# Turning gated tiles by DMA in the spatial stage instead of on TensorE in the last stage

## The chip, the cores and the metric

The kernel runs on one core of a Trainium2 chip. The core has TensorE (PE in the profile; PEld is its weight load), VectorE (DVE), ScalarE (ACT), GpSimd (POOL) and SyncE (SP, which here only issues DMAs). ACT and POOL issue DMAs too. The metric is the device time of one execution in microseconds. Before the change it is 636.57 us, the median of 3 runs (636.25 to 636.86).

## The reference

All arithmetic is in float32; S = 2048 rows, D = 512, H = 32 heads of 16, Fh = 688. With xn the normalised rows of x, the result is x + A(xn) + B(xn):

```python
def _A_ref(x, wqkv, w_phi, wo):          # linear attention
    q, k, v = heads of x @ wqkv
    phi = lambda t: concat(softmax(t @ w_phi), softmax(-t @ w_phi))   # per head
    kv, z = sum_s phi(k) v, sum_s phi(k)
    o = phi(q) kv / (phi(q) z + 1e-6)
    return o @ wo

def _B_ref(x, w_in, w_sp, b_sp, w_out):  # gated MLP with spatial mixing
    z = gelu(x @ w_in)
    z1 = z[..., :Fh]
    z2 = layernorm(z[..., Fh:])
    g = w_sp @ z2 + b_sp[:, None]        # over the 2048 rows
    return (z1 * g) @ w_out
```

The change is in B, between the product z1 * g and its multiplication with w_out.

## The kernel before

**Tiles and precision.** Rows go in 16 tiles of 128. Nearly every float32 product is made of three matmuls: both operands are split into a rounded high part and a rest (`round_h` on ACT, `rest_l` on DVE), and `mm3` adds high x high, high x low and low x high in PSUM.

**Stages.** First the input projections, the attention features and sums, and z1 before its GELU, which is stored to DRAM (`z1_d`). Then z2 with GELU and norm, split into the right-hand operands B, which stay in SBUF. Then the *spatial stage*: g = w_sp @ z2, for 8 pairs of row tiles (i = 0 to 7), each with four blocks of the inner dimension (n = 4i to 4i + 3), by a seven-product scheme in place of eight. The products P1, P2, P6, P5, P7, P3, P4 run in this order in every block, six matmuls each, and accumulate over the four blocks in seven PSUM buffers. There are eight such buffers (`psg`, tag "g"), taken in turn, so the first product of the next pair has a free one and the second needs the one that P1 of this pair held.

**What feeds TensorE in that stage.** `load_a` (SP's queue, line 516) loads weights of a block three blocks ahead, `prep_a` makes its left-hand operands with ACT roundings and DVE sums and rests; two sets alternate.

**The gate of a pair.** When the pair's last block is issued, `drain` (line 704) reads the seven PSUM buffers into the tile `c`: one ACT copy first (line 709), seven DVE operations after it. `gate` (line 719) then takes the GELU of z1 in place on ACT (line 722), multiplies by `c` on DVE (724), and writes, for the 48 remainder columns that do not fill a tile of 128, a rounded part and a rest side by side (727 to 729). Two DMAs on POOL's queue store the pair to DRAM (`u_d`, line 731). `load_z1` (line 687, POOL's queue) fetches the z1 of the next pair. The tiles `z1`, `c` and `rh` come from the pool `gt` with one buffer per name, so a name's next tile waits for all readers of the last one. The gate of the last pair runs in the last stage, after the iteration `GATE_LAST = 8`, and its `c` comes from another pool.

**The last stage.** For each row tile: load the gated tile (SP, line 746), turn it in blocks of 128 columns on TensorE into PSUM (`gate_T`, lines 749 to 761: five blocks and the 96 remainder columns), split the result into high and rest, multiply by w_out (`project_u`, line 885), add the attention output times wo (`project_o`, line 898), add x, store. Two tiles make an iteration; the tiles of a following iteration are turned in the current one. DVE also finishes the attention features of later tiles here, and POOL's queue copies them (line 836).

**Order.** Within an engine, instructions stand in an order that a planner lays down when the program is built: it plays the program through with its own costs and starts what is ready, earlier program order first. `tc.issue_after(x)` keeps instructions behind x on the same engine. At run time every engine and every DMA queue takes its instructions strictly in that order.

Of the kernel before, what the change touches and what calls it, by code (L numbers as in the profile page):

```python
# [11 lines left out]
F32R = mybir.dt.float32r  # L12
AF = mybir.ActivationFunctionType
# [12 lines left out]
KF = FH // P  # L26
REM = FH - KF * P
# [10 lines left out]
def mixer(ctx: ExitStack, tc: tile.TileContext, x, x_t, wv, wqkT, phi_bd, wo, w_in, wst, b_r, w_out, out):  # L38
# [32 lines left out]
    u_d = dram.tile([NT, P, FH + REM], F32, name="u_d")  # L71
# [615 lines left out]
    def load_z1(i):  # L687
        t = gt.tile([P, 2, FH + REM], F32, tag="z1", name="z1t")
        for k in range(2):
            pool.dma_start(t[:, k, :FH], z1_d[2 * i + k])  # L690
        return t
# [27 lines left out]
    def gate(i, cb, z):  # L719
        cb, first, _ = cb  # L720
        with tc.issue_after(first):
            act.activation(z[:, :, :FH], z[:, :, :FH], AF.Gelu_apprx_tanh)
        zs = z[:, :, :FH].rearrange("p k (j f) -> p k j f", j=2)
        dve.tensor_tensor(zs, zs, cb.rearrange("p (k j) f -> p k j f", k=2), op=ALU.mult)
# [4 lines left out]
        dve.tensor_copy(z[:, :, rm], rh.bitcast(F32))  # L729
        for k in range(2):  # L730
            pool.dma_start(u_d[2 * i + k], z[:, k])  # L731
# [13 lines left out]
    def load_u(i, t):  # L745
        sp.dma_start(t.bitcast(F32), u_d[i])
        return t

    def gate_T(ps, tag, z, h, l, rt):
        pt = ps.tile([P, 4, P], F32, tag=tag, name="ptu")  # L750
        for c in range(4):
            pe.transpose(pt[:, c].bitcast(F32R), z[:, c * P:(c + 1) * P], ident_r)
        round_h(act, h[:, :4], pt)
        rest_l(l[:, :4], pt, h[:, :4])
        pt = ps.tile([P, 4, P], F32, tag=tag, name="ptu2")
        pe.transpose(pt[:, 0].bitcast(F32R), z[:, 4 * P:5 * P], ident_r)
        lasts[2] = pe.transpose(pt[:2 * REM, 1].bitcast(F32R), z[:, KF * P:KF * P + 2 * REM], ident_r).ins
        round_h(act, h[:, 4:], pt[:, :1])
        lasts[1] = rest_l(l[:, 4:], pt[:, :1], h[:, 4:])
        lasts[0] = act.activation(rt, pt[:2 * REM, 1], AF.Copy).ins  # L760
        return h, l, rt
# [4 lines left out]
    def first_gate(i):  # L766
        a, b = slot("u_uh", F32R), slot("ul_rt", F32R)
        u = load_u(i, a[:, :FH + REM])
        return gate_T(psg, "g", u, k_tiles(a[:, FH + REM:]), k_tiles(b[:, :KF * P]), b[:2 * REM, KF * P:(KF + 1) * P])

# [18 lines left out]
    for n in range(NC):  # L789
# [21 lines left out]
        if n == NC - 2:  # L811
            us = {1: load_u(1, slot("u1", F32R)[:, :FH + REM])}
# [12 lines left out]
    def fetch_u(i):  # L825
        return load_u(i, cw.tile([P, FH + REM], F32R, tag="u", bufs=4, name="u"))
# [11 lines left out]
    def gated(z, ps=None):  # L838
        return gate_T(*(ps or (pst, "tr")), z, wk.tile([P, KF, P], F32R, tag="uh", name="uh"),
                      wk.tile([P, KF, P], F32R, tag="ul", name="ul"), wk.tile([2 * REM, P], F32R, tag="rt", name="rt"))  # L840

    kvT = cw.tile([P, 2 * NG, QP], F32, name="kvT")
    with tc.issue_after(cb[1]), tc.issue_after(cb[2]):
        uT.append(gated(us.pop(1), (psg, "g")))
# [40 lines left out]
    def project_u(i, u):  # L885
# [5 lines left out]
        for ds, p in parts:  # L891
            for c in range(KF):
                mm3(p, (uh[:, c], ul[:, c]), tuple(w[:, ds] for w in wu[c]), c == 0, False)
            for w in wu[KF]:
                pe.matmul(p, rt, w[:, ds], start=False, stop=False)  # L895
# [12 lines left out]
    GATE_LAST = 8  # L908
# [24 lines left out]
    for i in range(0, NT, 2):  # L933
# [56 lines left out]
```

## Time and profile before

| | |
|---|---|
| Runs | 636.25 to 636.86 us, median 636.57 (3 runs) |
| Profiled execution | 636.23 us, span 634.5 us |
| Busy, whole span | PE 629.0, PEld 571.1, DVE 509.0, ACT 267.9, POOL 114.9 us |
| Granted TensorE clock | 1.00 |
| DMA | 103.95 MB, mean 164 GB/s |

A row of a timeline gives the start, the busy time, the engine, the source line, the operation, what it writes and reads, the number of instructions merged, and in brackets how long the engine had stood idle before and what ended that. Matmuls of one engine overlap in the records, since they are pipelined: their pace is read from the starts. Rows with a "q" behind the engine's name are issues of DMAs, and "us to landing" is from issue until the data are there. A source line can be a helper's: L45 is `round_h`, L49 is `rest_l`, L53 to L55 are the three matmuls of `mm3`.

### The profile page before, as it was taken

What the parts mean: (1) busy time and instruction counts of PE and PEld (TensorE: products, weight loads), DVE (VectorE), ACT (ScalarE), POOL (GpSimd) and SP (SyncE); (2) the same over time, 40 slices, a digit from 0 to 9 for tenths busy, and PEclk for the clock granted to TensorE, in tenths of its full rate; (3) what the DMA queues carried; (4) which work ended last, traced back from release to release, by engine and by line L of the source; (5) the groups of instructions that cost most, each with busy time, mean ns of one, the idle gap of its engine ahead of it and who ended that gap; (6) DMA issues with size and microseconds to landing.
All of it is one profiled execution on the core that took longest, in us unless ns stands there. A gap on an engine that the chain in (4) does not pass through costs nothing.

```text
span 634.5 us, 11639 instructions
## 1 busy us (share of the span) xinstructions
PE 629.0 (99%) x4471; PEld 571.1 (90%) x4471; DVE 509.0 (80%) x941; ACT 267.9 (42%) x447; POOL 114.9 (18%) x195
## 2 busy tenths in 40 slices
PE   9999999999999999999999999999999999999997
PEld 7888888888888999999999999999999888888886
DVE  5979989998888578889987869678695698989521
ACT  5623334332433437887453434434353423323330
POOL 4542231322101005441011010000100200101000
PEclk9999999999999999999999999999999999999999
DMA  9477676666544941002464352543548877775620
GB/s 334 150 170 163 181 186 142 190 154 151 178 136 112 298 153 67 2 1 68 145 191 131 121 180 71 174 132 119 184 143 275 267 267 283 243 263 219 205 67 35
DMA packets 41908, 103.95 MB, mean 164 GB/s; under 512 B 5404, under 2 KB 6940, under 8 KB 41852
## 3 DMA queue, kind: packets, MB, share of 16 engines
q1 hardware_dynamic: 28524, 58.37, 28.7%
q0 software_dynamic: 10736, 38.67, 21.3%
q10 hardware_dynamic: 2592, 6.16, 2.6%
q8 instruction: 35, 0.57, 0.4%
q14 instruction: 21, 0.17, 0.1%
HBM read 62.01 MB, written 26.50 MB: 139 GB/s over the span
## 4 chain that ended last, share of the span: by engine, by line
PE 96%; DVE 3%; issue 0%; ACT 0%
PE g L54 11%; PE g L55 11%; PE g L53 11%; PE proj L53 6%; PE zps L53 6%; PE proj L55 6%; PE proj L54 6%; PE zps L55 6%; PE zps L54 6%; PE pout L53 6%; PE pout L54 5%; PE pout L55 5%; PE ptq L863 1%; PE po L877 1%; PE kvps L319 1%; PE pout L895 1%
## 5 line engine op out<-in xcount | busy, mean ns | idle before, releaser
L54 PE MATMUL g<-B,A 128*128 128x344 f32 x448 | 143.3, 320 | 0.0
L53 PE MATMUL g<-B,A 128*128 128x344 f32 x448 | 143.2, 320 | 0.0
L55 PE MATMUL g<-B,A 128*128 128x344 f32 x448 | 143.0, 320 | 0.0
L54 PEld LDWEIGHTS g<-B,A 128*128 128x128 f32 x448 | 84.2, 188 | 0.0
L53 PEld LDWEIGHTS g<-B,A 128*128 128x128 f32 x448 | 84.2, 188 | 0.0
L55 PEld LDWEIGHTS g<-B,A 128*128 128x128 f32 x448 | 84.1, 188 | 0.0
L49 DVE TENSOR_TENSOR A<-S,A 128x512 fp32r<-128x512 f32 x64 | 43.8, 688 | 29.8 <-ACT A L45 29.0
L45 ACT ACTIVATE A<-S 128x512 fp32r<-128x512 f32 x64 | 40.2, 631 | 60.5 <-PE g L55 37.1
L113 ACT ACTIVATE e<-e,r_x 128x1024 f32<-128x1024 f32 x32 | 36.8, 1149 | 46.0 <-DVE e L112 44.1
L53 PE MATMUL proj<-wqk_h,xT 128*128 128x512 f32 x124 | 49.6, 400 | 0.0
L45 ACT ACTIVATE A<-wf 128x512 fp32r<-128x512 f32 x64 | 33.3, 520 | 37.3 <-PE g L55 32.9
L55 PE MATMUL proj<-wqk_h,xT 128*128 128x512 f32 x124 | 48.8, 394 | 0.0
L54 PE MATMUL proj<-wqk_l,xT 128*128 128x512 f32 x124 | 48.7, 393 | 0.0
L115 DVE TENSOR_REDUCE sm<-e 128x64 f32<-128x1024 f32 x32 | 38.6, 1212 | 9.7 <-ACT e L113 9.4
L53 PE MATMUL zps<-w_h,xT 128*128 128x344 f32 x128 | 41.8, 326 | 0.4 <-ACT z1f L143 0.3
L55 PE MATMUL zps<-w_h,xT 128*128 128x344 f32 x128 | 40.9, 319 | 0.0
L54 PE MATMUL zps<-w_l,xT 128*128 128x344 f32 x128 | 40.8, 319 | 0.0
L49 DVE TENSOR_TENSOR A<-wf,A 128x512 fp32r<-128x512 f32 x64 | 35.4, 553 | 2.9 <-ACT A L45 2.5
L731 POOL DMA_DIRECT2D u_d<-z1t x16 | 8.7, 547 | 133.7 <-DVE A L49 93.8
L53 PE MATMUL pout<-wu,uh 128*128 128x512 f32 (+1 forms) x80 | 31.6, 395 | 0.0
L143 ACT ACTIVATE z1f<-zps,r_x 128x344 f32<-128x344 f32 (+1 forms) x30 | 17.0, 566 | 33.8 <-PE zps L55 33.3
L54 PE MATMUL pout<-wu,uh 128*128 128x512 f32 (+1 forms) x80 | 30.4, 380 | 0.0
(203 smaller groups left out, 1485.1 us busy)
## 6 DMA issues: line engine op xcount, KB each, us to landing
wf<-in_wst SPq DMA_DIRECT2D x64, 256.0 KB, 3.4
e_d<-e POOLq DMA_DIRECT2D x16, 544.0 KB, 4.1
et<-e_d SPq DMA_DIRECT2D x16, 544.0 KB, 5.0
zacc<-e POOLq DMA_DIRECT2D x16, 512.0 KB, 4.9
er<-et POOLq DMA_DIRECT2D x12, 512.0 KB, 4.0
u_d<-z1t POOLq DMA_DIRECT2D x16, 368.0 KB, 4.4
u<-u_d SPq DMA_DIRECT2D x15, 368.0 KB, 3.0
z_d<-z1f ACTq DMA_DIRECT2D x16, 344.0 KB, 3.8
```

Of the source, the lines that this page charges most:

```text
L45: return act.activation(h, src, AF.Copy).ins
L49: return (eng or dve).tensor_tensor(l, src, h.bitcast(F32), op=ALU.subtract).ins
L53: pe.matmul(dst, ah, bh, start=start, stop=False)
L54: pe.matmul(dst, ah, bl, start=False, stop=False)
L55: return pe.matmul(dst, al, bh, start=False, stop=stop).ins
L113: softmax_pair.exp = act.activation(e, e, AF.Exp, scale=scale).ins
L115: dve.tensor_reduce(sm, heads(e), axis=AX.X, op=ALU.add)
L143: z1_raw.last = act.activation(z[:, k], p, AF.Copy, scale=r_x[:, s:s + 1]).ins
L319: ins = pe.matmul(kv_acc[k:k + QP, m // 4], vs[:, m * QP:(m + 1) * QP], e[:, m * HP:(m + 1) * HP], start=s == 0 and m < 4, stop=s == NT - ...
L731: pool.dma_start(u_d[2 * i + k], z[:, k])
L863: pe.transpose(pt[:, a, k].bitcast(F32R), src, ident_r)
L877: lasts[3] = pe.matmul(po[r][c * QP:(c + 1) * QP, j // NG], kvT[rows, j], fs[j // 2][rows, j % 2], start=True, stop=True).ins
```

## The change

The gated tile is turned before it is stored. A float32 value is taken as two 16-bit halves. In `gate`, two ACT copies separate the low and the high halves of both row tiles into two planes; the planes lie in the tile `c`, which has been read by then. For each of the two row tiles a transposing DMA on SP's queue (`dma_start_transpose`) turns the 12 blocks of 128 x 128 halves into a tile "T", a POOL copy interleaves the halves again into the z1 tile, and the store follows as before, on POOL's queue. The tile is padded with zeros from 736 to 768 columns (UP), by a POOL memset ahead of each z1 load. In the last stage a load brings the turned tile; `gate_T` with its six TensorE transposes per tile is replaced by `gate_parts`, which splits the loaded tile with one ACT rounding, one DVE rest and one ACT copy of the remainder. Two ordering hints change with it, and `GATE_LAST` goes from 8 to 6; there the planes of the last pair have a tile of their own.

```diff
+UP = (KF + 1) * P
...
-    u_d = dram.tile([NT, P, FH + REM], F32, name="u_d")
+    u_d = dram.tile([NT, P, UP], F32, name="u_d")
...
     def load_z1(i):
-        t = gt.tile([P, 2, FH + REM], F32, tag="z1", name="z1t")
+        t = gt.tile([P, 2, UP], F32, tag="z1", name="z1t")
+        pool.memset(t[:, :, FH + REM:], 0.0)
...
+    def halves(ap):
+        return ap.bitcast(U16).rearrange("p (n two) -> p two n", two=2)
+
-    def gate(i, cb, z):
+    def gate(i, cb, z, planes):
...
+        planes = planes.bitcast(U16).rearrange("p (k two n) -> p k two n", k=2, two=2)
         for k in range(2):
+            act.activation(planes[:, k], halves(z[:, k]), AF.Copy)
+        for k in range(2):
+            t = gt.tile([P, 2, KF + 1, P], U16, tag="T", name="uT")
+            sp.dma_start_transpose(t.rearrange("p two b t -> p (two b) t"), planes[:, k].rearrange("p two n -> p (two n)"))
+            pool.tensor_copy(halves(z[:, k]), t.rearrange("p two b t -> p two (b t)"))
             pool.dma_start(u_d[2 * i + k], z[:, k])
...
-    def gate_T(ps, tag, z, h, l, rt):
...
+    def gate_parts(u, h, l, rt):
+        full = slice(0, KF * P)
+        round_h(act, h, u[:, full])
+        lasts[1] = rest_l(l, u[:, full], h)
+        lasts[0] = act.activation(rt, u[:2 * REM, KF * P:], AF.Copy).ins
+        return k_tiles(h), k_tiles(l), rt
...
         if n % NQ == NQ - 1 and i < NP - 1:
-            gate(i, drain(i, g, gt.tile([P, 4, FC], F32, tag="c", name="c")), z)
+            c = gt.tile([P, 2 * UP], F32, tag="c", name="c")
+            gate(i, drain(i, g, c[:, :2 * FH].rearrange("p (a b) -> p a b", a=4)), z, c)
...
-    GATE_LAST = 8
+    GATE_LAST = 6
...
         if i + 3 < NT:
-            with tc.issue_after(lasts[3]):
-                nxt[i + 3] = gated(us.pop(i + 3))
+            nxt[i + 3] = gated(us.pop(i + 3))
...
-                gate(NP - 1, cb, z)
+                gate(NP - 1, cb, z, gt.tile([P, 2 * UP], F32, tag="pl", name="pl"))
```

More of the change, by code (lines that the diff above doesn't have):

```diff
@@ L745, in load_u @@
     def load_u(i, t):
-        sp.dma_start(t.bitcast(F32), u_d[i])
+        sp.dma_start(t, u_d[i])
         return t
-    def gate_T(ps, tag, z, h, l, rt):
[L750 to L761, printed above, removed]
+    def gate_parts(u, h, l, rt):
[4 more added lines that the diff above has]
+        return k_tiles(h), k_tiles(l), rt
     def k_tiles(ap):
```

21 lines of the change are left out of this document (11 added, 10 removed).

## The prediction

> **What bounds the kernel now.** I read the page first, then the busy time by stage, then TensorE in order of time around the operations that go, and last the three queues through which a gated tile passes. All durations are of the profiled execution: 636.23 us, of which 634.5 is its span; the median of the three runs, 636.57, lies 0.34 higher.
>
> ```profile
> span 634.5 us, 11639 instructions
> PE 629.0 (99%) x4471; PEld 571.1 (90%) x4471; DVE 509.0 (80%) x941; ACT 267.9 (42%) x447; POOL 114.9 (18%) x195
> PE 96%; DVE 3%; issue 0%; ACT 0%
> ...
> 381.50:408.00 26.50, 26.50 (x170) 26.50 (x169) 20.41 (x44) 10.88 (x19) 2.16 (x4) 1.00 0.43 135
> 568.00:585.00 17.00, 17.00 (x120) 13.79 (x119) 15.75 (x32) 6.36 (x13) 1.07 (x3) 1.00 0.62 228
> 585.00:602.00 17.00, 17.00 (x120) 13.76 (x119) 9.87 (x16) 5.12 (x12) 2.16 (x4) 1.00 0.66 228
> ```
>
> The last three rows are one pair of the spatial stage and two pairs of the last stage (busy us of PE, PEld, DVE, ACT, POOL, then granted clock, DMA share, GB/s). TensorE has no hole in either, at clock 1.00, and the chain of waits is 96% TensorE. So a matmul removed shortens the run by its slot, and anything that makes TensorE wait lengthens it in full. DVE in the last stage has 17.00 - 15.75 = 1.25 us a pair to spare, so a gain of more than that would be cut off there.
>
> **What is removed: 96 transposes, six for each of 16 tiles.** Matmuls overlap in the records, so I go by starts.
>
> ```profile
> 585.57 0.63 PE L895 MATMUL pout<-wu,rt 96*128 96x512 f32 x2
> 586.58 1.09 PE L877 MATMUL po<-f,kvT 64*32 64x256 f32 x32
> ...
> 590.96 0.40 PE L55 MATMUL pout<-wu,ul 128*128 128x512 f32 x1
> 591.19 0.63 PE L895 MATMUL pout<-wu,rt 96*128 96x512 f32 x2
> 591.65 0.46 PE L752 MATMUL ptu<-zb,u 128*128 128x128 f32 x4
> 591.95 0.25 PE L756 MATMUL ptu<-zb,u 128*128 128x128 f32 x1
> 592.03 0.23 PE L757 MATMUL ptu<-zb,u 128*96 128x128 f32 x1
> 592.10 0.47 PE L53 MATMUL pout<-woh,oT 128*128 128x512 f32 x1
> 592.41 0.39 PE L54 MATMUL pout<-wol,oT 128*128 128x512 f32 x1
> ...
> 619.47 0.63 PE L895 MATMUL pout<-wu,rt 96*128 96x512 f32 x2
> 620.03 1.09 PE L877 MATMUL po<-f,kvT 64*32 64x256 f32 x32
> ```
>
> A 512-column matmul takes a slot of 591.19 - 590.96 = 0.23 us. From the remainder pair at 591.19 to the second output matmul at 592.41 go 1.22 us; three slots alone are 0.69, so the six transposes cost 0.53, the slower first matmul behind them included. Where the attention products follow, 585.57 to 586.58 is 1.01; at 619.47, where nothing is left to turn, it is 0.56: 0.45. Half of the tiles are of each kind: 8 x 0.98 = **7.8 us saved**. That is 0.98 a pair, under DVE's 1.25, and ACT and DVE do one split in place of two, so I take it whole. The tiles now loaded are 768 columns wide instead of 736; those loads have a pair's time and cost nothing.
>
> **What is added, and where it lies.** In the spatial stage each pair gets two ACT copies into the planes, two transposing DMAs on SP's queue, two POOL copies back, and the stores wait for all that. None is on TensorE. But they form a ring: the z1 tile, the tile c (now also the planes) and the turned tile T exist once each, so the next pair's z1 load waits for this pair's stores, the second transpose waits for the first POOL copy, and the next drain's first write to c waits for the second transpose. What it runs through now:
>
> ```profile
> 382.26 0.46 ACT L709 ACTIVATE c<-g 128x344 f32<-128x344 f32 x1 [0.48 <-PE g L55]
> 390.05 1.58 DVE L724 TENSOR_TENSOR z1t<-z1t,c 128x1376 f32<-128x1376 f32 x1
> 394.92 0.20 DVE L729 COPY z1t<-rh 128x96 f32<-128x96 f32 x1
> 395.66 1.08 POOL L731 DMA_DIRECT2D u_d<-z1t  x2 [18.73 <-DVE A L49]
> 402.03 1.08 POOL L690 DMA_DIRECT2D z1t<-z_d  x2 [5.28 <-issue]
> 408.72 0.46 ACT L709 ACTIVATE c<-g 128x344 f32<-128x344 f32 x1 [0.48 <-PE g L55]
> ```
>
> ```profile
> 302.38 1.19 POOL L690 DMA_DIRECT2D z1t<-z_d  x2 [10.80 <-PE g L55]
> 303.04 0.44 ACT L709 ACTIVATE c<-g 128x344 f32<-128x344 f32 x1
> 308.01 1.36 ACT L722 ACTIVATE z1t<-z1t 128x1376 f32<-128x1376 f32 x1 [0.99 <-DMA z1t<-z_d]
> 314.18 1.58 DVE L724 TENSOR_TENSOR z1t<-z1t,c 128x1376 f32<-128x1376 f32 x1
> 317.65 0.20 DVE L729 COPY z1t<-rh 128x96 f32<-128x96 f32 x1
> ```
>
> The ring in terms, from the gate's multiply to the next: multiply to the last DVE copy's end 5.07 us (390.05 to 395.12), or 3.67 in the first pair (314.18 to 317.85), I take 4.4; to the first store's issue 0.54; stores to z1 load 6.37; load to GELU 5.63 (302.38 to 308.01, where GELU waited for the DMA); GELU 1.36. Sum 18.3 against a period of 408.72 - 382.26 = **26.46**: 8.2 us are free.
>
> Now the additions on this ring. ACT's first plane copy, 1536 columns: 1.36 x 1536/1376 = 1.5, plus 0.3 for half of a rounding ahead of it in ACT's order. Pad 0.1. One store issue less at the end, -0.5. Together 1.4. Then twice a transpose T and twice a POOL copy C, which the trace does not show:
>
> ```profile
> u<-u_d SPq DMA_DIRECT2D x15, 368.0 KB, 3.0
> raw<-nm_d POOLq DMA_DIRECT2D x11, 256.0 KB, 6.3
> ...
> L49 POOL TENSOR_TENSOR w_l<-wrow,w_h 128x688 fp32r<-128x688 f32 x4 | 6.7, 1677 | 4.0 <-ACT w_h L45 4.0
> L170 POOL MEMSET zacc<- 128x1024 f32 x1 | 0.9, 942 | 0.0
> L163 POOL TENSOR_SCALAR_AFFINE_SELECT mask<-mask 128x256 f32<-128x256 f32 x2 | 0.9, 449 | 0.1
> masks.py:199 POOL TENSOR_SCALAR_AFFINE_SELECT ident<-ident 128x128 f32<-128x128 f32 x1 | 0.3, 284 | 0.1
> ```
>
> T moves 384 KB. Not below 3.0, the plain load of 368 KB on the same queue; above, 6.3, the slowest group to land. I take 3.4, near the plain load, as queue and bytes are alike and two-byte pieces can only add. C is 1536 elements with one read and one write: at the memset's rate 1.4; at the two-input operation's 1536/688 x 1.68 = 3.7; by the two one-input rows 1.29 ns a column, 0.28 + 1408 x 0.00129 = 2.1, which I take as the nearest.
>
> The Trainium skill bears on T. "DMA: Bandwidth & Descriptors", section "Latency and other measured facts", gives 261 GB/s for transposing DMAs and section "Anatomy of one DMA" a fixed 2 us: an estimate of 3.5 for T, and by it the sum below would be 1.2 us higher. No trace here shows it.
>
> **The sum.** The ring becomes 18.3 + 1.4 + 2 x (3.4 + 2.1) = 30.7 us, 4.2 more than the period: the gate slips 4.2 us later with every pair. What does a late gate hold up? Not the stores' readers, they come much later, but c. With the multiply at M, c is free at M + 4.4 + 1.8 + 2T + C = M + 15.1; the next drain is due at M + 26.46 - 7.79 = M + 18.7, so 3.6 early. Behind a late drain stand the PSUM banks: there are eight and a pair holds seven, in product order, so TensorE runs the rest of the last block (six products) and the first product of the next pair before it needs the bank of P1. 170 matmuls in 26.50 us are 0.156 each, a product 0.94, seven 6.6; less the 0.46 of the drain's first copy and some interleaved work, 5.5. Reserve: 9.1 us of lateness.
>
> The first pair starts late: 314.18 - 303.04 = 11.1 against 390.05 - 382.26 = 7.8, so 3.4. Drains of pairs 1 to 6 hang on c (the last drain has a tile of its own), so five slips count: 3.4 + 5 x 4.2 = 24.4, less 9.1, leaves TensorE **waiting 15.3 us** in the second half of the spatial stage. 636.23 - 7.8 + 15.3 = 643.7, and with the median's 0.34, **644.0**.
>
> What else waits. SP's queue stands at a transpose until ACT has the plane; behind it are the loads of the spatial weights:
>
> ```profile
> SPq L516 <- DVE S L534: 79.8, 22, 4.2
> wf<-in_wst SPq DMA_DIRECT2D x64, 256.0 KB, 3.4
> ```
>
> SP mostly waits there for buffers; a load comes two blocks (2 x 6.6 us) ahead of its use and takes 3.4, so some 9 us may go by: nothing, unless both transposes stand in one row. ACT's roundings behind a plane copy have a block of reserve. POOL copies and DVE get in each other's way:
>
> ```profile
> L311 DVE TENSOR_TENSOR e<-e x16: 1208/1220/2018, 30.1 to 201.4; 128x1024 f32<-128x1024 f32 x16
> 30.13 2.02 DVE L311 TENSOR_TENSOR e<-e 128x1024 f32<-128x1024 f32 x1
> ...
> 29.39 1.68 POOL L49 TENSOR_TENSOR w_l<-wrow,w_h 128x688 fp32r<-128x688 f32 x1
> 31.02 1.54 POOL L88 TENSOR_TENSOR r_x<-mv_x,mhalf 128x1 f32<-128x1 f32 x1
> ```
>
> The DVE operation that began beside the POOL subtraction took 2.02 instead of 1.22 and ended 1.1 after it, and the tiny POOL operation behind took 1.54. So a pair's two copies can take 2 x 2.1 from DVE's 26.50 - 20.41 = 6.1 of slack: it fits. The last pair's gate, one iteration (17 us) earlier in the last stage, is 1.4 + 11.0 = 12.4 longer and lands in time.
>
> **Rivals.**
> *The ring still closes (faster).* With X = T + C, the wait is about 12X - 50 us: it equals the 7.8 saved at X = 4.8 and is nothing at 4.2. The lower ends, 3.0 + 1.4 = 4.4, leave 3, and with the first pair's shorter DVE tail nothing: 628.4 to 634. For it: the planner may pull the gate's small DVE operations together once they are late; both low bounds are real rows. Against: each must be at its bound.
> *The transpose is dear (much slower).* T = 5 gives X = 7.1, a wait of some 35 and 663; T = 6.3 gives 50 and 678. For: no operation here moves two-byte pieces. Against: nothing on a hardware queue takes that long for such a size. Beside it stands the page "VectorE: DVE Perf Modes", section "The three transpose paths", with 1309 ns for one 128x128 bf16 block through the DMA; twelve in a row would be 15.7 us for T, an estimate, and some 150 us on the run. No run here shows it.
> *Weight loads late behind SP's head.* Both transposes and the copy between them hold SP for 2T + C = 8.9, just the reserve; with a DMA slower by one, each of seven pairs loses 1 to 2 us: 636 to 643 with the gain.
> *A wash.* A wait of 6.5 to 9 cancels the gain.
>
> **How the numbers follow.** Forecast 0.41 (own range 638 to 658: X up to 6.7), ring closes 0.37, dear transpose 0.12, late loads 0.04, wash 0.06. Below 0.2% (1.27 us) a measurement of this kernel tells nothing. Faster 0.37; same 0.06; slower 0.57. The range takes in the closed ring whole and the dear transpose up to T = 5.7: 628 to 672.
>
> **What would show it.** Transposes gone from the last stage and a pair there at 16.0 us: the saving. Successive z1 loads more than 26.5 us apart, the drain's first copy waiting for a transpose instead of TensorE, and holes in TensorE from the third or fourth pair on: the ring. T from issue to landing and C by their own rows. If z1 loads stay 26.5 apart, my ring is too long and the run is near 628.5; if TensorE waits for A, it is the loads or DVE.

## The result, and the profile after

The changed kernel takes **686.0 us** (median of 4 runs, 685.35 to 687.21) where the kernel before, on the same chip, takes 636.41 (636.18 to 636.86): a ratio of 1.078 [1.0762, 1.0799], 49.6 us slower. The forecast of 644.0 had the direction and one of the two places; the size was far off, outside the range of 628 to 672.

The profile after has a span of 683.7 us, 49.2 more than before. First, the spatial stage and the rest in windows of the two kernels, before and then after (us, then busy time and number of instructions by engine, granted clock, DMA share, GB/s):

```profile
282.00:494.10 212.10, 212.10 (x1351) 212.06 (x1350) 171.63 (x360) 96.02 (x165) 20.61 (x39) 1.00 0.46 148
494.10:634.50 140.40, 136.88 (x969) 111.36 (x968) 96.81 (x168) 43.25 (x98) 10.63 (x21) 1.00 0.58 203
```

```profile
282.00:533.30 251.30, 222.51 (x1346) 221.00 (x1346) 183.65 (x362) 115.07 (x180) 44.73 (x58) 0.93 0.50 141
533.30:683.70 150.40, 134.52 (x879) 105.35 (x878) 97.14 (x150) 45.39 (x83) 19.59 (x27) 0.94 0.66 209
```

The spatial stage has the same matmuls (about 1350) and is 39.2 us longer. The last stage has some 90 PE instructions less, as it should, and is 10.0 us *longer* instead of 7.8 shorter. The waits of the changed kernel, ACT's for c and then the two of TensorE that lead its list (waiter, what it waited for: us in all, times, longest):

```profile
ACT c L712 <- DMA uT<-c: 31.0, 6, 9.6
...
PE g L55 <- ACT c L712: 28.8, 5, 8.7
PE po L883 <- ACT f L871: 11.7, 2, 7.0
```

The first two lines are the chain of the prediction: TensorE's product waits for the drain's first copy, which waits for c, which a transpose still reads. The third is not in the prediction. Nor is another part of the 39.2 us: TensorE waits for 28.8 of them, and the other 10.4 are matmuls that ran slower at a lower granted clock (PE busy 222.51 us instead of 212.10; see the last section).

One whole ring of the changed kernel follows, pair 3, in the timelines of POOL, ACT, DVE and SP (start, duration in us, engine, line, operation, and in brackets the idle time before it):

```profile
406.01 1.07 POOL L693 DMA_DIRECT2D z1t<-z_d  x2 [0.31 <-issue]
424.69 2.23 POOL L742 COPY z1t<-uT 128x1536 uint16<-128x1536 uint16 x1 [17.61 <-DMA uT<-c]
427.23 0.55 POOL L743 DMA_DIRECT2D u_d<-z1t  x1 [0.30 <-POOL z1t L742]
434.39 1.91 POOL L742 COPY z1t<-uT 128x1536 uint16<-128x1536 uint16 x1 [6.62 <-DMA uT<-c]
439.94 0.15 POOL L691 MEMSET z1t<- 128x64 f32 x1 [2.79 <-DMA u_d<-z1t]
440.41 1.07 POOL L693 DMA_DIRECT2D z1t<-z_d  x2 [0.31 <-issue]
```

```profile
410.84 0.42 ACT L47 ACTIVATE A<-wf 128x256 fp32r<-128x256 f32 x1 [0.32 <-PE g L57]
411.17 1.34 ACT L728 ACTIVATE z1t<-z1t 128x1376 f32<-128x1376 f32 x1
...
419.40 2.84 ACT L738 ACTIVATE c<-z1t 128x1536 uint16<-128x1536 uint16 x2
```

```profile
413.10 1.58 DVE L730 TENSOR_TENSOR z1t<-z1t,c 128x1376 f32<-128x1376 f32 x1
...
418.66 0.21 DVE L735 COPY z1t<-rh 128x96 f32<-128x96 f32 x1
```

```profile
420.89 1.46 SPq L741 DMA_TRANSPOSE uT<-c  x1
423.85 6.06 SPq L518 DMA_DIRECT2D wf<-in_wst  x3
430.00 1.45 SPq L741 DMA_TRANSPOSE uT<-c  x1
```

From one z1 load to the next 440.41 - 406.01 = 34.4 us pass, where 26.46 is the period. The second transpose could have gone at 426.92, when the first copy gave T free; it stands in SP's queue behind three loads of spatial weights and goes at 430.00. And the GELU came up in ACT's order right behind a rounding of A that had waited for TensorE.

Over the stage, the z1 loads of pairs 1 and 6 (POOL's timeline of the changed kernel) give the mean ring:

```profile
339.39 1.07 POOL L693 DMA_DIRECT2D z1t<-z_d  x2 [0.31 <-issue]
...
511.13 1.07 POOL L693 DMA_DIRECT2D z1t<-z_d  x2 [0.31 <-issue]
```

The drain's first copy of pair 6 gives the lateness (ACT's timeline, changed kernel and then the kernel before):

```profile
505.68 0.46 ACT L712 ACTIVATE c<-g 128x344 f32<-128x344 f32 x1 [5.37 <-DMA uT<-c]
```

```profile
461.66 0.46 ACT L709 ACTIVATE c<-g 128x344 f32<-128x344 f32 x1 [0.48 <-PE g L55]
```

(511.13 - 339.39) / 5 = **34.35 us a ring**; the last drain that hangs on c is 44.0 us late, and the stage is 39 longer: 5 us were reserve.

The last stage of the changed kernel in the timelines of PE (its two holes), ACT and SP:

```profile
547.49 1.08 PE L883 MATMUL po<-f,kvT 64*32 64x256 f32 x8 [4.67 <-ACT f L871]
...
555.59 2.06 PE L883 MATMUL po<-f,kvT 64*32 64x256 f32 x24 [7.02 <-ACT f L871]
```

```profile
554.94 1.57 ACT L871 ACTIVATE f<-ptq 128x512 f32<-128x512 f32 x3 [7.50 <-DMA u_d<-z1t]
```

```profile
527.88 4.78 SPq L741 DMA_TRANSPOSE uT<-c  x1
532.76 0.53 SPq L853 DMA_DIRECT2D kvT<-kvT_d  x1
533.38 4.86 SPq L753 DMA_DIRECT2D wof<-in_wo  x8
538.56 2.58 SPq L758 DMA_DIRECT2D u<-u_d  x4
541.25 4.39 SPq L741 DMA_TRANSPOSE uT<-c  x1
```

ACT's copy to f waits for the *store of pair 6's gated tile*: the last stage's tiles lie in memory of the spatial stage, and that is not free before the last store has read z1. The store is late because the gate is, and pair 6's turns are slow here. The POOL copies that wait for them show it (POOL's timeline):

```profile
537.13 1.94 POOL L742 COPY z1t<-uT 128x1536 uint16<-128x1536 uint16 x1 [2.69 <-DMA uT<-c]
...
550.00 1.88 POOL L742 COPY z1t<-uT 128x1536 uint16<-128x1536 uint16 x1 [8.49 <-DMA uT<-c]
```

From issue to copy the first turn takes 9.3 us (527.88 to 537.13) and the second 8.8, beside the loads of the last stage. Between the first copy's end and the second turn's issue, 2.2 us more go by on SP's queue behind those loads.

### The profile page after: what moved, and what is told of

Same layout as the page of the kernel before. It is cut to its first block, busy times and chain, and to the rows that moved or that the text cites. A ratio compares the mean times of both kernels' runs of the same rounds, so it can differ in the third digit from the quotient of the medians.

```text
span 683.7 us, 11512 instructions
## 1 busy us (share of the span) xinstructions
PE 637.1 (93%) x4375; PEld 573.9 (84%) x4375; DVE 521.5 (76%) x925; ACT 288.8 (42%) x447; POOL 147.4 (22%) x219
## 4 chain that ended last, share of the span: by engine, by line
PE 81%; DMA 7%; DVE 6%; ACT 3%; issue 1%; POOL 1%; SPq 0%; ACTq 0%; POOLq 0%
PE g L55 9%; PE g L56 8%; PE g L57 8%; DMA uT<-c 6%; PE proj L55 6%; PE zps L55 6%; PE proj L57 6%; PE proj L56 6%; PE zps L57 6%; PE zps L56 6%; PE pout L55 5%; PE pout L56 5%; PE pout L57 5%; PE po L883 1%; DVE A L51 1%
## 5 line engine op out<-in xcount | busy, mean ns | idle before, releaser
L55 PE MATMUL g<-B,A 128*128 128x344 f32 x448 | 147.7, 331 | 28.8 <-ACT c L712 28.8
L56 PE MATMUL g<-B,A 128*128 128x344 f32 x448 | 147.1, 329 | 0.0
L57 PE MATMUL g<-B,A 128*128 128x344 f32 x448 | 146.7, 328 | 0.0
L55 PEld LDWEIGHTS g<-B,A 128*128 128x128 f32 x448 | 87.7, 196 | 30.2 <-ACT c L712 30.2
L56 PEld LDWEIGHTS g<-B,A 128*128 128x128 f32 x448 | 87.8, 196 | 0.0
L57 PEld LDWEIGHTS g<-B,A 128*128 128x128 f32 x448 | 87.4, 195 | 0.1
L742 POOL COPY z1t<-uT 128x1536 uint16<-128x1536 uint16 x16 | 31.9, 1993 | 175.6 <-DMA uT<-c 141.4
L47 ACT ACTIVATE A<-wf 128x512 fp32r<-128x512 f32 (+1 forms) x64 | 33.3, 521 | 39.1 <-PE g L57 33.0
L55 PE MATMUL proj<-wqk_h,xT 128*128 128x512 f32 x124 | 49.6, 400 | 0.0
L55 PE MATMUL zps<-w_h,xT 128*128 128x344 f32 x128 | 41.8, 326 | 0.4 <-ACT z1f L145 0.3
L51 DVE TENSOR_TENSOR A<-wf,A 128x512 fp32r<-128x512 f32 (+1 forms) x64 | 35.4, 554 | 4.1 <-ACT A L47 3.8
L711 DVE SCALAR_TENSOR_TENSOR c<-g,bias,c 128x344 f32<-128x344 f32 x32 | 17.9, 571 | 22.6 <-ACT c L712 22.5
L55 PE MATMUL pout<-wu,uh 128*128 128x512 f32 (+1 forms) x80 | 31.7, 396 | 0.0
L145 ACT ACTIVATE z1f<-zps,r_x 128x344 f32<-128x344 f32 (+1 forms) x30 | 17.0, 566 | 33.8 <-PE zps L57 33.2
```

The costliest lines, as they stand in the source:

```text
L47: return act.activation(h, src, AF.Copy).ins
L51: return (eng or dve).tensor_tensor(l, src, h.bitcast(F32), op=ALU.subtract).ins
L55: pe.matmul(dst, ah, bh, start=start, stop=False)
L56: pe.matmul(dst, ah, bl, start=False, stop=False)
L57: return pe.matmul(dst, al, bh, start=False, stop=stop).ins
L145: z1_raw.last = act.activation(z[:, k], p, AF.Copy, scale=r_x[:, s:s + 1]).ins
```

## The experiments

The kernels are named by what they change. "Ring" is the distance of the z1 loads of pairs 1 and 6, a fifth of it; "stage" is from the first to the last start of the product line of g (row L55, or L53 where the lines are those of before), from starts given to a tenth.

| kernel | time, us | ratio to before | ring | stage | TensorE's main wait in the stage |
|---|---|---|---|---|---|
| before | 636.4 | | 26.0 | 211.9 | none |
| changed | 686.0 | 1.078 [1.0762, 1.0799] | 34.4 | 250.9 | c, 28.8 |
| e1 no turn | 630.2 | 0.990 [0.9886, 0.9918] | | 211.6 | none |
| e2 half turn | 632.2 | 0.993 [0.9907, 0.9942] | 26.1 | 211.5 | none |
| e3 turn into z1 | 667.7 | 1.049 [1.0469, 1.0502] | 29.5 | 228.4 | c, 11.3 |
| e4 fill | 691.3 | 1.087 [1.0847, 1.089] | 35.9 | 257.9 | c, 14.3 |
| e8 ring by POOL | 698.5 | 1.098 [1.0953, 1.101] | 35.9 | 243.6 | c, 18.1 |
| e6 stores last | 687.5 | 1.082 [1.079, 1.0846] | 34.6 | 251.7 | c, 30.4 |
| e6b stores last | 683.0 | 1.073 [1.071, 1.0742] | 34.3 | 249.8 | c, 27.2 |
| e10 last pair plain | 673.4 | 1.057 [1.0551, 1.0595] | 34.5 | 251.0 | c, 30.2 |
| e12 turns overlap | 672.4 | 1.056 [1.0546, 1.0577] | 33.7 | 242.0 | c, 20.2 |
| e15 GELU earlier | 670.0 | 1.052 [1.0504, 1.0537] | 31.7 | 241.2 | A, 16.5 |
| e19 GELU first | 664.8 | 1.044 [1.0422, 1.0457] | 30.2 | 239.2 | A, 15.8 |
| e18 changed, earlier | 700.4 | 1.102 [1.0961, 1.1071] | 35.8 | 262.7 | c, 32.9 |
| e9 half by TensorE | **634.5** | 0.997 [0.996, 0.998] | 26.2 | 211.3 | none |
| e13 twelve tiles | 661.2 | 1.038 [1.0362, 1.0396] | 33.8 | 242.0 | c, 20.7 |
| e14 ten tiles | 655.9 | 1.031 [1.0292, 1.0325] | 31.0 | 227.2 | c, 8.9 |
| e17 twelve, earlier | 662.3 | 1.041 [1.0392, 1.0423] | 31.6 | 240.7 | A, 16.5 |

**What is the saving worth, and is the ring the cause?** The changed kernel without the turns (tiles are stored unturned, so this part of the computation is left out), and with one turn of a pair only (the other tile is stored unturned):

```diff
 # e1: neither transpose nor POOL copy     # e2: both only for k == 0
-            t = gt.tile([P, 2, KF + 1, P], U16, tag="T", name="uT")
-            sp.dma_start_transpose(...)
-            pool.tensor_copy(halves(z[:, k]), t...)
             pool.dma_start(u_d[2 * i + k], z[:, k])
```

> The changed kernel without the transposing DMAs and without the POOL copies: the planes are still written, the pair is stored as it is (so the turning itself is left out of the computation). Ring theory (the one-buffer ring z1 load, GELU, multiply, planes, turn, copy back, store, next z1 load sets the pace of the spatial stage): without 2T + 2C, 12 us or more, the ring of some 35 us falls under the period of 26.5; no TensorE wait in the spatial stage, 636.4 - 7.8 = 628.6 us. If the plane copies, the wider stores or the changed order cost something by themselves: 630 to 640.

> The changed kernel with the turn and the POOL copy for the first row tile of each pair alone; the second is stored unturned (left out of the computation). Ring theory: the second transpose (about 5 us from issue to landing) and its copy (1.95) with their hand-overs leave the ring, 35 - 7.5 = 27 to 28 us against 26.5, a slip of about 1 us a pair, inside the reserve of 9: no or hardly any TensorE wait, 628 to 633 us. Rival (the transposing DMAs themselves, their traffic and the clock, each cost their share wherever they stand): half of the 57 us between 628.6 and 686 remains, 657 us.

Measured: 630.18 (629.89 to 630.82) and 632.2 (630.68 to 632.26). The 96 transposes are worth **6.3 us** on the time, not 7.8. Pairs run at 16.0 us as forecast, but in two places of the last stage TensorE's transposes had stood between the features' transposes and `po`, which needs ACT's copy f: from `ptq` to the end of `po` 3.16 us pass before and 3.19 without them. That time had been covered, and now is a wait. At a third place, where two tiles had been turned, TensorE now waits 0.7 us for ACT's oT. With one turn a pair, TensorE waits nowhere in the stage and the loads stand 26.1 apart. So eight of these transposes running beside TensorE cost it nothing here: it is the length of the chain that counts.

**The chain shortened by its copies.** Transposes write into z1, the tile goes out as two planes, and ACT puts them together in the last stage:

```diff
-            t = gt.tile([P, 2, KF + 1, P], U16, tag="T", name="uT")
-            sp.dma_start_transpose(t..., planes[:, k]...)
-            pool.tensor_copy(halves(z[:, k]), t...)
+            sp.dma_start_transpose(z[:, k].bitcast(U16)..., planes[:, k]...)
...
+        act.activation(halves(v), u.bitcast(U16)..., AF.Copy)   # in gate_parts
```

> The whole turn, all 16 transposing DMAs, in a shorter ring: they write the turned planes straight into the z1 tile (its values are in the planes by then), so that both can be in flight together and no POOL copy stands in the ring; the planes are stored as they are and an ACT copy in the last stage interleaves the halves (1.5 us a tile, ACT is busy 5 to 7 of 17 us a pair there). Ring theory: 35 less two copies (4) less most of the second transpose (4 to 5) is 26 to 27 us, about the period, and the tile c is free about 4 us before the next drain: 628 to 634 us. Rival (the transposing DMAs themselves cost): near 686 us, since all are there.

Measured: 667.7, missed by 34. The ring closed only to 29.5, and the stage is still 16.5 longer. In the last stage ACT's interleave costs 1.92 us a tile and TensorE waits more for ACT there. The expectation took the rest of the ring to stay as forecast. It did not: from GELU to the first plane copy 10.7 us passed in most pairs. The GELU itself waited for its load here.

**Is it the clock?** TensorE restarts at half clock after the holes (last section). Useless matmuls into the unused columns of a bank keep it busy:

```diff
+            if name == "P1" and n % NQ == 0 and i > 3:
+                for _ in range(56):
+                    pe.matmul(g[name][:, FC:], ah[:, 0], bh[:, :D - FC], start=False, stop=False)
```

> The changed kernel with 56 useless matmuls of 168 columns (into columns of a PSUM buffer that nothing reads) behind the first product of pairs 4 to 7, that is where TensorE stands and waits for the drain. If the waits also cost by the clock (the granted clock is 0.5 for 7 to 10 us after each of them, and matmuls start 0.29 apart instead of 0.158), a TensorE kept busy keeps its clock and the stage gets about 8 to 10 us shorter though it has more to do: 676 to 678 us. If the half clock is only a record of the waits themselves: 686 us or, as far as the matmuls do not fit in the holes, up to 692.

Measured: 691.3, with a stage of 257.9 and a clock of 0.97 in it (0.93 in the changed kernel). More clock, no gain; but the run does not settle what the half clock costs. The useless matmuls took 6.4 us a pair where TensorE would have waited, and the ring grew to 35.9, mainly because the planner set the GELU of pairs 3 and 4 behind 8 roundings of A instead of 5 (load to GELU 8.6 us in both, 5.2 and 4.7 in the changed kernel). That the half clock lies inside the wait for the ring is argued, not shown.

**A ring without any transpose.** The kernel before, with nine POOL copies of the tile onto itself between gate and store:

```diff
+        if i < NP - 1:
+            for _ in range(9):
+                pool.tensor_copy(z[:, :, :FH], z[:, :, :FH])
```

> The kernel before, with no transpose anywhere added: nine POOL copies of the gated tile onto itself (no change of values) stand between gate and store of every pair but the last. I expect 1.6 to 2.0 us each, 14 to 18 us a pair, so a ring of some 33 to 37 us. Here c is free right after the multiply, so TensorE's reserve is about 22 us instead of 9. Ring theory: the z1 loads stand one ring apart, the gate slips by (ring - 26.46) a pair, and TensorE waits 3.4 + 5 x (ring - 26.46) - 22 us in the spatial stage: at 34.5 some 22, time about 658 (at 33, 650; at 37, 671), and more where the last pair's late gate also holds up the last stage. Rival (the loss of the changed kernel comes from the transposing transfers themselves or from SP's queue): no transpose here, so 636 to 638.

Measured: 698.5 (697.46 to 701.54). The rival's 636 to 638 is refuted: with no transpose and no new work on SP, the same kind of wait is there. Its waits of PE:

```profile
PE ptq L866 <- ACT rt L763: 20.0, 1, 20.0
PE g L53 <- ACT c L709: 18.1, 5, 5.8
```

The nine copies take 14.1 us a pair, the loads of pairs 2 to 5 stand 31.8 apart, and the size was missed by a new thing. The GELU of pair 1 came 24.7 us behind its load (timelines of POOL and ACT):

```profile
340.25 1.08 POOL L690 DMA_DIRECT2D z1t<-z_d  x2 [5.79 <-issue]
```

```profile
364.57 0.42 ACT L45 ACTIVATE A<-wf 128x256 fp32r<-128x256 f32 x1 [0.32 <-PE g L55]
364.90 1.34 ACT L722 ACTIVATE z1t<-z1t 128x1376 f32<-128x1376 f32 x1
```

It does not wait for the load there; it stands in ACT's order behind a row of roundings that go at TensorE's pace. The planner's order has it there. That place alone adds some 18 us of lateness (the loads of pairs 1 and 2 stand 50.0 apart), so the run shows that a long ring brings the wait without a transpose, but not how much of the 18.1 us is due to the copies. The half of its loss that lies in the last stage (the stage is 31.7 longer, the run 62.1) was not followed up.

**The last stage.** Pair 6 alone is stored unturned (its turn is left out of the computation):

```diff
+            if i != NP - 2:
                 t = gt.tile(...)      # transpose and copy as before
```

> Changed kernel, but the tiles of pair 6 are stored unturned (turning them is left out). Theory: the spatial stage stays at 250 to 252 us, since nothing in it waits for this pair's gate, but the gate ends some 16 us sooner, the last stage's f tiles get their memory in time, and TensorE's wait for f of 11.7 us goes with the half clock behind it: the last stage 133 to 136 instead of 150.4, time 670 to 673. Rival (the last stage is long for another reason, as the turned loads or ACT's order): 683 to 687.

Measured: 673.4 (670.83 to 674.18), at the upper end of the 670 to 673 expected. The stage stays (251.0), the wait for f is gone, and in its profile the rest of the span is

```profile
533.50:669.10 135.60, 129.32 (x879) 103.00 (x878) 97.55 (x152) 45.24 (x83) 15.13 (x23) 1.00 0.68 226
```

135.6 us against 150.4, at full clock. The late gate of one pair costs the last stage 14.8 us in the profiles (12.6 by the medians).

**What makes the second turn slow?** Both stores behind both turns. In the first form the planner put the first store back to where it was, so that kernel changed nothing but the line:

> Changed kernel, but both stores of a pair are issued after both turns, so that no store runs beside the second transpose. If the store beside it is what makes the second transpose slow: it lands in 4.0 to 4.4 us instead of 5.0 to 6.7 from the first copy's end, the ring shortens by about 1 us (from 34.4 to 33.4), the spatial stage by about 5 us, time 679 to 682. Rival (the second transpose is slow in itself, or by the weight loads on its queue): it stays at 5 us or more, and the time at 685 to 689.

Measured: 687.5, like the changed kernel. The form that ties the stores behind the second copy:

```diff
-            pool.tensor_copy(halves(z[:, k]), t...)
-            pool.dma_start(u_d[2 * i + k], z[:, k])
+            turned = pool.tensor_copy(halves(z[:, k]), t...)
+        with tc.issue_after(turned.ins):
+            for k in range(2):
+                pool.dma_start(u_d[2 * i + k], z[:, k])
```

> Changed kernel with both stores of a pair tied behind the second POOL copy (in e6_stores_last the first store was still issued right behind the first copy, as in the changed kernel, so that run changed nothing). If the store beside it slows the second turn: from its issue to the copy's start it takes 4.0 to 4.4 us instead of 5.3, the ring 33.3 instead of 34.4, the spatial stage 246 instead of 251, time 679 to 683. Rival (slow for another reason, as the weight loads on SP's queue): 5 us or more, time 685 to 690.

Measured: 683.0 (681.68 to 683.57). From the second turn's issue to its copy 4.5 us pass in the mean of five pairs, 5.3 in the changed kernel. The means hide two cases. In pairs 2 and 5 of the changed kernel the second turn goes right behind the first copy, with the store beside it all the way, and takes 6.7 and 6.2. In pairs 3 and 4 it stands 3.1 us behind weight loads on SP's queue; the store has nearly landed by then, and it takes 4.4. In e6b pair 2's takes 4.0 with no store beside it, so there the store cost 2.7 us; pair 5's takes 5.6 even so, so the store is not all. The ring hardly changed, at 34.25. With both stores at the end, 4.4 us instead of 3.6 pass from the second copy to the next z1 load, which takes back the 0.8; and from z1 load to GELU it takes 8.15 us instead of 6.27, while the multiply's DVE tail is 1.8 shorter.

**Both turns at once.** The first turn lands in the other half of z1, so the second does not wait for the first copy:

```diff
+            if k == 0:
+                t = z[:, 1].bitcast(U16).rearrange("p (two b t) -> p two b t", two=2, t=P)
+            else:
                 t = gt.tile([P, 2, KF + 1, P], U16, tag="T", name="uT")
             sp.dma_start_transpose(...)      # both, then both copies and stores
```

> Changed kernel, all else the same, but the first turn of a pair lands in the memory of the other half of z1 instead of in T, so that the second turn no longer waits for the first POOL copy: both turns run one behind the other. Ring theory: from the first turn's issue to the second copy's start 12.9 us become some 6.3, and the first turn waits 1.4 for the second plane; the ring goes from 34.4 to 29 us (28 to 30.5), c is free some 3 us sooner, and TensorE's wait in the spatial stage falls from 39 (stage stretch) to 3.4 + 5 x 2.7 - 8.7 = 8 us (3 to 13); the last stage, whose f tiles wait for pair 6's gate, loses 0 to 8 instead of 12. Time 642 (633 to 650). Rival (what costs is the number of transposes or copies, not their order): 683 or more.

Measured: 672.4 (671.59 to 672.88), missed by 30. c is indeed free sooner: from the multiply to the next drain 14.3 us instead of some 20. But the ring is 33.7 (POOL's timeline, pairs 1 and 6):

```profile
335.03 1.07 POOL L693 DMA_DIRECT2D z1t<-z_d  x2 [0.31 <-issue]
...
503.67 0.54 POOL L693 DMA_DIRECT2D z1t<-z_d  x1 [0.31 <-issue]
```

The shortening is there, and eaten at one place, as pair 3 shows in the timelines of POOL and ACT:

```profile
399.91 1.07 POOL L693 DMA_DIRECT2D z1t<-z_d  x2 [0.31 <-issue]
```

```profile
410.50 0.63 ACT L47 ACTIVATE A<-wf 128x512 fp32r<-128x512 f32 x1 [1.48 <-PE g L57]
412.39 0.63 ACT L47 ACTIVATE A<-S 128x512 fp32r<-128x512 f32 x1 [1.26 <-PE g L57]
414.26 0.63 ACT L47 ACTIVATE A<-S 128x512 fp32r<-128x512 f32 x1 [1.24 <-PE g L57]
415.21 0.42 ACT L47 ACTIVATE A<-wf 128x256 fp32r<-128x256 f32 x1 [0.31 <-PE g L57]
415.53 1.34 ACT L728 ACTIVATE z1t<-z1t 128x1376 f32<-128x1376 f32 x1
```

15.6 us from load to GELU, where a z1 load lands some 3.8 us after its issue (median). Each rounding waits for TensorE, and the GELU is behind them. In ACT's order there are 16 such roundings a pair. Between the drain's first copy and the GELU stand none in the kernel before, 3 or 4 where one tile is turned (e2, e9), 5 to 8 in the changed kernel, and mostly 9 to 12 here (pair 0, where it is 2 or 3 in all of these kernels, is not counted). The Trainium skill, "Perfetto Trace Analysis", section "Tensor Engine Instruction (MATMUL, LD_WEIGHTS)", says that ACT, DVE and GpSimd are strictly first in, first out; the rows agree, for the GELU starts with no idle time of its own right behind the last of them.

**The GELU moved forward.** It is tied ahead of the roundings of a later block, in the overlapped kernel (e15: 4 to 5 roundings behind the drain's copy; e19: 2 to 4) and in the changed kernel (e18: 1 or 2 in most pairs, 4 in pair 1):

```diff
-            act.activation(z[:, :, :FH], z[:, :, :FH], AF.Gelu_apprx_tanh)
+            pin.append(act.activation(z[:, :, :FH], z[:, :, :FH], AF.Gelu_apprx_tanh).ins)
...
+            with (tc.issue_after(pin.pop()) if pin and n % NQ == 0 else ExitStack()):   # e19: NQ - 1
                 A[n + 2] = prep_a(n + 2, raw.pop(n + 2))
```

> As e12_turns_overlap, and the GELU is tied ahead of the four or five roundings of A that prepare the third block after the drain: it stands 4 to 5 roundings behind the drain's first copy in ACT's order instead of 9 to 12. Order theory: in e12 the z1 load had landed some 7 us before the GELU came up in ACT's order (load to GELU 11.4 us against some 4.4 for issue and landing), so the ring goes from 33.7 to 27 us (26.5 to 28), the lateness stays within the reserve, TensorE waits 0 to 3 us in the spatial stage, and the time is 630 to 636. Rival (transposes beside other transfers are the cost, the GELU only follows): the ring stays at 32 us or more and the time above 665. A third way: roundings now behind a GELU that waits for its load keep TensorE from A, 640 to 655 with TensorE waiting for ACT's A.

> As e15, with the GELU tied one block earlier still (2 to 3 roundings behind the drain's copy). If the load's landing sets it, the ring is 26.5 to 27.5 as in e15 and the time the same within 2 us (630 to 636). If the GELU waits for its load with A's roundings behind it, TensorE waits for A: 636 to 650.

> The changed kernel, with nothing but the GELU tied as in e15 (1 to 2 roundings behind the drain's copy instead of 5 to 8). Here the z1 load itself is late, so the GELU gains only load to GELU 6.3 - 4.4 = 1.9 us of the ring: 34.4 to 32.5. c is held as long as before (20 us), so the spatial stage shortens by 5 x 1.9, from 251 to some 242, and the time is 672 to 678. If the order were the whole cause: below 650. If it does nothing: 684 to 688.

Measured: 670.0, 664.8 and 700.4, each more than 20 us above its forecast. From e12 over e15 to e19 the ring follows the GELU's place, 33.7, 31.7 and 30.2, and the whole fall is in the piece from load to GELU (11.4, 8.3 and 6.5 us; the rest of the ring is 22.4, 23.4 and 23.7). So the order accounts for the loss of e12 in part. But the time hardly gains, because the wait moved: PE's waits in e15 are mostly for A and little for c,

```profile
PE g L55 <- ACT A L47: 16.5, 5, 7.3
PE po L892 <- ACT f L880: 6.9, 2, 3.5
PE g L55 <- DVE c L711: 4.8, 2, 2.4
```

the "third way" of that expectation, though its time is above the 640 to 655 given there: what stands behind a GELU that waits is late itself. In e18 the theory fell altogether: the load-to-GELU piece shrank to 5.2 us, but the rest of the ring grew by 2.5 (the second turn stood 3.1 us behind SP's weight loads instead of 1.6, the DVE tail took 6.8 instead of 5.7, the first turn 4.6 instead of 4.0), and the kernel is 14 us slower than the changed one. Whether an order exists in which two turns a pair cost nothing stays open. A second buffer for z1, c or T, which would break the ring itself, was not tried.

**Fewer turns.** One tile of pairs 0 to 5 turned by DMA, the other ten tiles by TensorE as before:

```diff
+    TURN = lambda i: i % 2 == 0 and i < 12
...
+            if TURN(2 * i + k):      # plane copy, transpose, POOL copy; else store as it is
...
+        f = gate_parts if TURN(i) else gate_T      # in the last stage
-    GATE_LAST = 6
+    GATE_LAST = 8
```

> A version that may beat both: the first row tile of pairs 0 to 5 is turned by DMA, the other ten row tiles by TensorE in the last stage as before, and the last pair's gate stands where the kernel before has it. TensorE is rid of 36 of 96 transposes. Ring theory: one turn makes a ring of about 25.5 us, under the period of 26.46, so TensorE waits nowhere in the spatial stage, and the time falls by 36/96 of 6.3, 2.4 us, less what the shorter cover of the wait for f costs: 633.5 to 636. Rival (each transpose costs by itself): 640 or more.

Measured: **634.49** (634.14 to 634.94), ratio 0.997 [0.996, 0.998]: the one arrangement here with nothing left out that is faster than the kernel before, by 1.9 us or 0.3%, with no wait of TensorE in the stage. Ten and twelve tiles with overlapped turns, and twelve with the GELU tied as in e15:

> As e13, but row tiles 5 and 9 are turned by TensorE as well, so pairs 2 and 4 turn one tile (ring about 25.5) and pairs 0, 1, 3, 5 two (ring about 29). Ring theory: lateness at the last c 3.4 + 2.7 + 2.7 - 1 + 2.7 - 1 = 9.5 against a reserve of 8.7: a wait of at most 1 us. 60 transposes are worth 3.2 by e9: 633.2 to 634.5.

> Both row tiles of pairs 0 to 5 turned by DMA with the overlapped turns, pairs 6 and 7 by TensorE as before. By e9's saving (1.9 us for 36 transposes) 72 transposes are worth 3.8: 632.6 if the lateness stays inside the reserve. Ring theory with a ring of 29: lateness 3.4 + 5 x 2.7 = 17 against 8.7, so TensorE waits some 8 us and the time is 638 to 643; with a ring of 27.5 or less there is no wait and 632 to 634.

> As e13_twelve_tiles (pairs 0 to 5 turned by DMA, pairs 6 and 7 by TensorE), with the GELU tied as in e15. Order theory: no wait in the spatial stage, and 72 transposes less are worth 3.8 us by e9's rate: 632 to 634. Rival as for e15: 655 or more.

Measured: 655.9, 661.2 and 662.3, missed as e12 and e15 were. They show the graded effect: the more pairs turn both tiles, the longer the mean ring and the stage (none 26.2 and 211.3, four of them 31.0 and 227.2, six 33.8 and 242.0).

## Why the prediction was right and wrong

**Right**: what bounds the kernel, the ring through the single z1 buffer and c, the wait's place ("the drain's first copy waiting for a transpose instead of TensorE"), the direction, and the duration of POOL's copy (2.1 forecast, 2.0 measured). The transpose alone, 3.4 forecast, takes 4.0 to its copy.

The dear transpose (T of 5 or more) was not what happened to the first turn, though its time of 678 was nearer; the second turn, with 5.3 in the mean, and pair 6's turns, with 9.3 and 8.8, were dear. Against that rival I had read that nothing on a hardware queue takes so long for such a size. The profile of the kernel before says otherwise: wrow<-in_w_in, 344 KB on SP's queue, landed in 5.6 us, and single loads of 172 KB in 6.7 and 7.0, so that 6.3 was not the slowest either.

The estimate of 3.5 worked out from the Trainium skill, "DMA: Bandwidth & Descriptors", was near for the first turn; the fixed 2 us in it stand in its section "Anatomy of one DMA" for DMAs that GpSimd issues, while these go from SP, so that it came near shows no mechanism. The 15.7 from the Trainium skill's time of one block ("VectorE: DVE Perf Modes", section "The three transpose paths") did not come: twelve blocks in one DMA landed in 3.9.

**Wrong by 42 us** (span against span): 39 instead of 15.3 in the spatial stage, and +10.0 instead of -7.8 in the last stage. Of the latter 17.8, 1.5 is the saving that was 6.3, some 15 the late gate, and 1.5 is in no run's account. Two steps failed. The second transpose was priced like the first, with no wait for its issue; and pair 6's late gate was taken to hold up nothing in the last stage.

*The terms of the ring.* Means of the five rings from pair 1 to pair 6, us:

| step | forecast | measured |
|---|---|---|
| z1 load to GELU | 5.6 | 6.3 |
| GELU to multiply | 1.4 | 1.8 |
| multiply to last DVE copy's end | 4.4 | 5.7 |
| to the first transpose's issue | 1.8 | 2.1 |
| first transpose to its copy | 3.4 | 4.0 |
| first copy | 2.1 | 2.0 |
| to the second transpose's issue | 0 | 1.6 |
| second transpose to its copy | 3.4 | 5.3 |
| second copy | 2.1 | 1.9 |
| to the next z1 load | 6.5 | 3.6 |
| **ring** | **30.7** | **34.3** |

The slip of 4.2 a pair became 7.9, and five slips make 18 us of it. The second transpose and its wait on SP's queue are the step that was mis-sized: 6.9 us together instead of 3.4, which is 3.5 of the ring's 3.6. The other errors cancel by luck: five terms were too small by 0.3 to 1.3, together 3.3, the two copies too large by 0.1 and 0.2, and the last step, from the second copy to the next z1 load, too large by 2.9. I had taken the multiply's DVE tail as a mean of its best and its usual row, where the late pairs took more than the usual one; I set the second transpose equal to the first, though a store can run beside it; and I priced SP's queue from the loads' side only: that the loads wait for a transpose. That the second *transpose* stands behind loads which wait for buffers (1.6 us a ring: 3.1 in two pairs, 1.7 in one, nothing in two) is the same queue read the other way, and was missing.

*The hold of c.* From the multiply of pair 5 to the next drain 20.3 us (505.68 - 485.38), forecast 15.1: instead of 3.6 early, c is 1.6 late. That is the other 5 us. The second transpose and its wait lie in this stretch too.

*The clock.* The forecast counted waiting alone. Of the 39 us, 28.8 were waiting and 10.4 matmuls at half clock; the ring's account above gives the sum without a term of its own for the clock, but no run shows that the clock cost nothing.

*"The last pair's gate ... lands in time."* True for the very last pair; but pair 6's gate is late by the whole lateness of the ring, and the last stage cannot write the rest of its first f tiles before that gate's store has read z1. I followed c into the next drain and never asked who takes z1's memory after the stage. e10 shows it: without that gate's turns, 14.8 us of the last stage come back.

*The removal.* 96 transposes at 0.98 us a row tile were taken whole. Where they covered TensorE's wait for f, 1.5 us were not saved (e1).

**Behind the terms** lies what I treated as given: the order of ACT's queue. I read "GELU waits for the z1 load" off the first pair, where the trace says so; in the later pairs of the changed kernel it stands behind roundings, and its place is written by the planner. In the changed kernel this step is only 0.7 us above the forecast, and moving the GELU forward there made the run slower (e18). In e12 it ate most of what the overlap had gained (5.1 of 5.7 us a ring), and moved forward there it makes A late instead (e15, e19). That much is shown; the rule by which the planner sets the place is not, nor why e3, whose GELU waits for its load, still has a ring of 29.5.

## What to carry to other kernels

Work that is hidden behind a single buffer is priced by the whole ring of that buffer, from load to next load, with the places of its instructions in every in-order queue it crosses: here 8.2 us of slack became 7.9 of debt a pair, and debt adds up from pair to pair, so an error of 3.6 us in the ring is multiplied by the number of rounds. Two equal operations in a ring need not cost the same: ask for each what stands ahead of it in its queue and what runs beside it. Follow each buffer that comes free late beyond its own stage, too: the next user may be the next stage's memory. And where half of an edit fits into the slack (one turned tile a pair: loads 26.2 apart and no wait), do half: here a gain of 0.3%.

## What the runs showed of the hardware

**Half clock after a wait.** In the changed kernel every hole of over 4 us on TensorE is followed by a stretch at half clock; the first hole of the spatial stage, 2.06 us long, is not. In the changed kernel's PE timeline and its windows:

```profile
434.86 0.65 PE L55 MATMUL g<-B,A 128*128 128x344 f32 x1 [4.85 <-ACT c L712]
435.31 0.49 PE L56 MATMUL g<-B,A 128*128 128x344 f32 x1
435.60 0.49 PE L57 MATMUL g<-B,A 128*128 128x344 f32 x1
...
444.71 0.32 PE L57 MATMUL g<-B,A 128*128 128x344 f32 x1
444.87 0.32 PE L55 MATMUL g<-B,A 128*128 128x344 f32 x1
445.03 0.33 PE L56 MATMUL g<-B,A 128*128 128x344 f32 x1
```

```profile
433.50:440.00 6.50, 5.14 (x18) 5.14 (x19) 4.67 (x9) 1.72 (x3) 2.52 (x3) 0.50 0.23 79
```

After a hole of 4.85 us matmuls start 0.29 apart at a granted clock of 0.50, and 0.16 apart once it is back at 1.00. In five of the six holes of this kind the clock fell 3.1 to 3.5 us after TensorE fell idle (the sixth began while it was still low); in the spatial stage it rose again after 4.8 to 5.6 us of work. The Trainium skill, "TensorE: Matmul & The Clock Gate", section "Part 1: The HAM clock gate (the "warmup" mystery)", has the array fall to half clock after an idle window of about 3.4 us and rise after a busy one; the rows agree with the fall, and with the rise as far as that it came after work. In the spatial stage each such stretch but the last is followed by another wait for c, which may hide it; e4 does not settle that. In the last stage the half clock goes on for 4.3 us after the last hole, where no further wait can hide it.

**A transpose of 384 KB**, twelve blocks of 128x128 two-byte elements from one place of SBUF to another, was in the spatial stage issued in 1.3 to 1.6 us (once 2.4) and landed in 3.9 (median), 4.0 to the start of the copy that waits for it (first turns). Beside a store of the same size on POOL's queue the way to the copy was 6.7 in pair 2, and 4.0 without that store (e6b). In the last stage, beside its loads, the four turns of the changed kernel took 7.1 to 9.3 us to the copy, while its DMAs moved 244 to 280 GB/s in those stretches, against 141 at a first turn of the spatial stage (pair 3).
